# Turning a 128 x 512 map of k: TensorE transposes and ScalarE copies, or VectorE's 32 x 32 transposes

## The chip, the core and the metric

The kernel runs on one core of a Trainium2 chip. The metric is device time in microseconds of one execution; the number given for a kernel is the median of several executions. The engines have short names in the profile: PE is TensorE (PEld its weight loads), DVE is VectorE, ACT is ScalarE, POOL is GpSimd, SP is SyncE, which here only issues transfers. Each engine works through its own list of instructions in order, and a semaphore wait at the head of a list holds everything behind it on that engine.

## The reference

Input x is 2048 x 512. It is normalised per row (xn), and then two branches are computed and multiplied:

```
xn = layernorm(x)
q, k, v = xn@wq, xn@wk, xn@wv          # 32 heads of 16, 4 segments of 512 rows
per segment s, per head:
    a_dot = softmax(q k^T / 4 + causal mask) v
    a_mem = (phi(q) M) / (phi(q) z + 1e-6)      # phi(t) = t + 1 if t > 0 else exp(t)
    o     = g a_mem + (1 - g) a_dot             # g = sigmoid(beta), per head
    M    += phi(k)^T v ;  z += sum over rows of phi(k)
s_out = concat(o) @ wo
h     = relu(xn @ w1) @ w2               # w1 512 x 1792, w2 1792 x 512
out   = x + s_out * silu(h)
```

What matters for the change is the line for M. It sums over the rows of a segment, so on TensorE the rows have to lie on the partitions, for phi(k) as for v.

## The kernel before

All large products are split in two parts (`h` and `l` tiles) and are made of three matmuls each, in two halves of 64 partitions that run side by side in the array: the lower half at L742, the upper half at L750. One such pair of matmuls over 512 columns is called a step below. Weights are loaded by SP into `io` tiles, split by ACT (L408) and POOL (L409).

The four segments are cut into four groups of 8 heads each, so there are 16 groups n = 4s + g. For a group, `proj` computes q and k, `projout` splits them for a transfer to DRAM and back (`stack`), and makes phi of q and k (L982, L983 on ACT, L990 on DVE). Half a group (4 heads) at a time goes through `rowmax` (scores at L1144 on TensorE, their row maxima at L1150 on DVE, in five steps of PSUM tiles), `maxrows` (a 32-partition transpose of the maxima at L1168 on DVE and two transfers), `expo` (transposed scores at L1196, exponentials on ACT at L1207 and L1213) and `pv` (L1244). The feed-forward branch is the filler between these.

The work around the change is this. phi(k) of a group is a tile `pk` of 128 partitions (8 heads x 16) by 512 rows. `memory(n)` turns it into `pkT`, 128 rows on the partitions, four chunks of 128 columns. `memory2(n)` multiplies it with v (32 small matmuls at L1101) and adds the result into `mc` (L1106, L1109). The last segment needs no map, so `memory` works for 12 groups. Before the change it takes two PSUM banks, makes 8 TensorE transposes of 64 partitions (L1071, two side by side), and copies the two banks into `pkT` with two ACT instructions (L1077). There is one `pkT` buffer.

PSUM has eight banks: six general ones, taken one or two at a time by the steps, `rowmax`, `pv` and `memory`, and a pair `pt` for `expo` and `numden`.

What sets the order: the program first collects all work as a list of small entries (an entry is one call of `S.pe`, `act`, `dve`, `pool` or `dma`; `Tape.op` and `Tape.pe` only append to the list). Then `Tape.play` issues them in the order that the string ORDER writes out: each letter says which of the waiting entries, counted from the back of the list, comes next. The duration that a call carries (0.14 + 140 x 0.00105 us for a call of `dve` with 140 columns, say) is not used when the kernel is built; such durations belonged to the search that wrote the strings. CHOICES holds the yes and no decisions of the program (among them how many warming matmuls stand in the opening, and when a chain is flushed without a partner), BANKS the PSUM bank of each taking, PLAN the order of the weight loads.

## Time and profile before

| quantity | value |
|---|---|
| median of 3 executions | 704.0 us (703.73 to 704.62) |
| the profiled execution's own time | 705.35 us |
| its span, first to last instruction | 703.6 us |
| granted TensorE clock | 1.00 |
| PE busy | 688.4 us (98%) |
| DVE busy | 438.4 us (62%) |
| ACT busy | 415.6 us (59%) |
| POOL busy | 448.0 us (64%) |

The busy times are unions of instructions: two matmuls side by side count once. Matmul ends are modelled, so a busy PE is not PE at its peak, and a short wait can hide in it. A row of a group reads: line, engine, operation, tiles, shapes, count, then busy time and mean of one, then the idle time of that engine ahead of it and what ended it.

### The profile page before, as it was taken

Reading aid. Unit: us, or ns where it says so; the run is one execution under the profiler, and the core shown is the slowest. Engines: PE = TensorE matmul, PEld = TensorE weight load, DVE = VectorE, ACT = ScalarE, POOL = GpSimd, SP = SyncE. Lnnn points to the kernel's source line nnn. Section 1 sums busy time; section 2 is a strip of 40 time slices with the busy share of each in tenths; the row PEclk is TensorE's granted clock in tenths of the full one; section 3 lists DMA queues with packets and bytes.
Section 4 is the critical chain, followed back from the end, with each engine's and each line's share of the span. In section 5 each row is a group of like instructions: output and inputs, shape, how many; then the busy total and the mean of one; then the engine's idle time right before and its main releaser. Section 6 shows DMA issues by size and latency. Waiting matters only on the chain.

```text
span 703.6 us, 18639 instructions
## 1 busy us (share of the span) xinstructions
PE 688.4 (98%) x6866; PEld 554.8 (79%) x6866; DVE 438.4 (62%) x1399; ACT 415.6 (59%) x645; POOL 448.0 (64%) x571
## 2 busy tenths in 40 slices
PE   9999999999999999999999999999999999999996
PEld 7878788878877798787788769787777878877675
DVE  4078767675966666466666664765577447566156
ACT  5454656756765773665575676457557555664651
POOL 4561656555666657774775777578467666765575
PEclk9999999999999999999999999999999999999999
DMA  5786466556875578666477567867666787745334
GB/s 171 230 277 205 148 219 196 188 178 203 261 226 154 191 234 283 205 193 201 142 242 231 185 200 221 260 200 228 197 184 185 237 273 228 254 149 144 95 86 135
DMA packets 126451, 141.46 MB, mean 201 GB/s; under 512 B 24904, under 2 KB 70216, under 8 KB 126360
## 3 DMA queue, kind: packets, MB, share of 16 engines
q1 hardware_dynamic: 126152, 140.07, 64.5%
q8 instruction: 54, 0.88, 0.5%
q14 instruction: 37, 0.30, 0.1%
q10 hardware_dynamic: 208, 0.20, 0.1%
HBM read 99.01 MB, written 34.93 MB: 190 GB/s over the span
## 4 chain that ended last, share of the span: by engine, by line
PE 89%; DVE 4%; DMA 3%; ACT 2%; issue 1%; SPq 1%; POOL 0%; DVEq 0%; POOLq 0%; ACTq 0%
PE ps L742 48%; PE ps L750 14%; PE ps L1244 10%; PE ps L1144 6%; PE pt L1196 6%; DVE none L1150 1%; DVE F L1033 1%; ACT pq L1031 1%; DMA ks<-sdk 1%; PE pt L1023 1%; DMA dd<-rq 1%; PE ps L700 1%; PE ps L698 1%; PE ps L699 1%; DMA io<-in_A_wv_dram 1%
## 5 line engine op out<-in xcount | busy, mean ns | idle before, releaser
L1150 DVE CUSTOM_DVE_ANT_0 none<-ps,causal 128x512 bf16<-128x512 f32 (+3 forms) x512 | 250.2, 489 | 107.1 <-PE ps L1144 85.6
L409 POOL TENSOR_TENSOR wl<-io,wh 128x512 fp32r<-128x512 f32 x176 | 227.9, 1304 | 114.6 <-ACT wh L408 89.8
L1213 ACT ACTIVATE P<-pt 128x1024 f32<-128x1024 f32 x128 | 131.3, 1026 | 78.2 <-PE pt L1196 56.0
L750 PE MATMUL ps<-xl,wh 64*128 64x512 f32 x352 | 142.2, 404 | 0.0
L742 PE MATMUL ps<-xh,wh 64*128 64x512 f32 x352 | 141.6, 402 | 0.0
L750 PE MATMUL ps<-xh,wh 64*128 64x512 f32 x352 | 137.1, 389 | 0.0
L750 PE MATMUL ps<-xh,wl 64*128 64x512 f32 x352 | 137.0, 389 | 0.0
L742 PE MATMUL ps<-xl,wh 64*128 64x512 f32 x352 | 136.8, 389 | 0.0
L742 PE MATMUL ps<-xh,wl 64*128 64x512 f32 x352 | 136.7, 388 | 0.0
L408 ACT ACTIVATE wh<-io 128x512 fp32r<-128x512 f32 x176 | 106.9, 626 | 41.7 <-PE ps L750 20.3
L1203 POOL TENSOR_SCALAR_AFFINE_SELECT P<-P 128x512 f32<-128x512 f32 x128 | 80.4, 644 | 39.5 <-ACT P L1213 26.8
L742 PE MATMUL ps<-wh,hh 64*128 64x512 f32 x224 | 91.3, 408 | 0.3 <-DVE md L1150 0.3
L750 PE MATMUL ps<-wl,hh 64*128 64x512 f32 x224 | 90.7, 405 | 0.0
L750 PE MATMUL ps<-wh,hl 64*128 64x512 f32 x224 | 87.3, 390 | 0.0
L750 PE MATMUL ps<-wh,hh 64*128 64x512 f32 x224 | 87.2, 389 | 0.0
L742 PE MATMUL ps<-wl,hh 64*128 64x512 f32 x224 | 87.2, 389 | 0.0
L742 PE MATMUL ps<-wh,hl 64*128 64x512 f32 x224 | 87.1, 389 | 0.0
L1144 PE MATMUL ps<-ks,qs 64*128 64x256 f32 (+3 forms) x512 | 74.1, 332 | 3.5 <-issue 1.4
L1244 PE MATMUL ps<-P,vt 128*17 128x512 f32 (+3 forms) x1024 | 75.2, 434 | 0.0
L742 PEld LDWEIGHTS ps<-xh,wl 64*128 64x128 f32 x352 | 65.0, 185 | 8.1
L1196 PE MATMUL pt<-qs,ks 64*128 64x384 f32 (+3 forms) x512 | 67.6, 312 | 3.9 <-DVE F L1033 2.6
L742 PEld LDWEIGHTS ps<-xh,wh 64*128 64x128 f32 x352 | 65.2, 185 | 7.6 <-issue 1.7
(181 smaller groups left out, 1720.8 us busy)
## 6 DMA issues: line engine op xcount, KB each, us to landing
io<-in_B_w_dram SPq DMA_DIRECT2D x112, 256.0 KB
qs<-sdq SPq DMA_DIRECT2D x32, 512.0 KB
ks<-sdk SPq DMA_DIRECT2D x32, 512.0 KB
sdq<-F SPq DMA_DIRECT2D x16, 512.0 KB
sdk<-F SPq DMA_DIRECT2D x16, 512.0 KB
io<-in_A_x_dram SPq DMA_DIRECT2D x28, 256.0 KB
io<-in_A_wv_dram SPq DMA_DIRECT2D x16, 256.0 KB
io<-in_A_wq_dram SPq DMA_DIRECT2D x16, 256.0 KB
```

Of the source, the lines that this page charges most:

```text
L408: act(512, [rk], [hk], lambda: ACT.activation(h, raw, AF.Copy), 7.0 + nsplit if early else 6.0)
L409: pool(512, [rk, hk], [lk], lambda: POOL.tensor_tensor(l, raw, r32(h), op=OP.subtract), 8.5 + 1.3 * nsplit if early else 25.4)
L698: PE.matmul(pt, st_, mv_, start=first, stop=False)
L699: PE.matmul(pt, st_, ml, start=False, stop=False)
L742: i = PE.matmul(m[0], m[2][0][LO], m[2][1][LO], start=m[4], stop=False)
L750: PE.matmul(h[0], h[2][0][HI], h[2][1][HI], start=False, stop=h[5] is not None)
L1144: PE.matmul(two[a][0][:, o:o + w], qs[r, p, w - 128:w], ks[r, p, :w], start=True, stop=True)
L1150: dve(w + 40 + TTR, [pk, "causal"], [f"{dk}.{p}{a}{j}"], lambda p=p, j=j, o=o, w=w, a=a, pS=pS: DVE.tensor_tensor_reduce(none[:, :w], pS[: ...
L1196: PE.matmul(pT[:, a, o:o + w], ks[r, p, 128 * i:128 * i + 128], qs[r, p, 128 * i:], start=True, stop=True)
L1203: pool(512, ks, ks, lambda: POOL.affine_select(t, t, pattern=[[0, 4], [1, 128]], compare_op=OP.is_ge, fill=0.0, base=0, channel_multiplier ...
L1213: act(1024, tk, [both[p]], lambda: ACT.activation(P[:, 2 * p:2 * p + 2, :], pT, AF.Exp, scale=0.25), 18.5)
L1244: PE.matmul(pO[32 * b:32 * b + 17, 128 * i:], v, P[:, b, o:o + w], start=i == 0, stop=i == 3)
```

## The change

`memory(n)` no longer asks for PSUM banks. In place of the 8 TensorE transposes and 2 ACT copies it issues 16 DVE transposes. Each reads 32 partitions of `pk` (32 features, b = 0 to 3) by 128 columns (32 rows out of each of the four chunks, picked by a = 0 to 3) and writes 32 partitions of `pkT`, in four blocks of 32 x 32. Each has its own key, so that `memory2` waits for all 16. The content of `pkT` is the same.

The four strings are written anew. PLAN is as long as before (176 loads, a few changed in place). BANKS has 909 entries instead of 933, 24 fewer, which is two for each of 12 maps. ORDER has 4,014 entries instead of 3,858, 156 more; 12 x (16 - 1 - 2) is 156, since the 8 TensorE transposes were one entry. The first 96 decisions of CHOICES, which take in all those on warming matmuls in the opening (19 times yes, 20 times no), are the same bit for bit.

```diff
@@ -55,62 +55,63 @@
 CHOICES = (
-    "fffbc60001aab2ab2abaaeaafa01041efb7ac3ac75dd9f77b3f6f3d023beeee2773b38ef73bf773fe5f7cf9e815f7def7bb3b9d8ee0f2777"
...
+    "fffbc60001aab2ab2abaaeaaba01041ebedd93ac75ddbdbecbf67c5ddc082777673bb1cef73bfef79f95fbcf8fbdeeabbe1dd8eee87f0fbbb"
...
 PLAN = (
-    "IJKLQAERSTUVefghBFWXCGYZijklDHabcdmnopAEQRqrSBFIJKLTUVCefghGWXDHMNOPYZijklaAEbcdmnopQRBFqrSTIJKLUVefghCGWXMNOPDH"
+    "IJKLQAERSTUVefghBFWXYCGZijklDaHbcdmnopAEQRqrSBFIJKLTUVCGefghWXYDHMNOPZijklabAEcdmnopBFQRqrSTIJKLUVefghCGWXMNOPDH"
     "YZijklaAEbcdmnopBFQRqrSTIJKLCGMNOPUVefghDHWXYZijklabcdmnopqrMNOP")
...
@@ -1062,25 +1063,18 @@
         if s == NSEG - 1:
             return
         pk, fk, zs, z = PK.pop(n)
-        yield ask(*fk, 2)
-        two = PDR.take(2)
-
-        def go():
-            for c in range(4):
-                for (pt, _), r in zip(two, HALF):
-                    PE.transpose(pt[:, 64 * c:64 * c + 64], pk[r, 128 * c:128 * c + 128], ident[r, r])
-
-        S.pe(T64, fk, [k for _, k in two], go)
         assert not PKTS
         pkT, tk = PKT.next()
-        for (pt, pk_), r in zip(two, HALF):
-            act(256, [pk_], [tk], lambda pt=pt, r=r: ACT.activation(
-                pkT[:, :, r], pt[:, :256].rearrange("p (c f) -> p c f", c=4), AF.Copy), 0.0)
-        PKTS[n] = (pkT, tk, zs, z)
-        yield 0.45, False
+        tks = [f"{tk}.{a}{b}" for a in range(4) for b in range(4)]
+        pv = pk.rearrange("p (t a j) -> p a t j", a=4, j=32)
+        for i, k in enumerate(tks):
+            a, b = slice(32 * (i // 4), 32 * (i // 4) + 32), slice(32 * (i % 4), 32 * (i % 4) + 32)
+            dve(140, fk, [k], lambda a=a, b=b, i=i: DVE.transpose(pkT[a, :, b], pv[b, i // 4]), 4.0)
+        PKTS[n] = (pkT, tks, zs, z)
+        yield 0.0, False
 
     def memory2_needs(n):
-        return [PKTS[n][1], *(f"v{vbuf(n)}{c}" for c in range(4))], [PDR.two()[0][1]]
+        return [*PKTS[n][1], *(f"v{vbuf(n)}{c}" for c in range(4))], [PDR.two()[0][1]]
```

## The prediction

> **What bounds the kernel now.** I read the page's sums and its chain first, then the busy times of TensorE by stretch, then what TensorE waits for.

> ```profile
> span 703.6 us, 18639 instructions
> PE 688.4 (98%) x6866; PEld 554.8 (79%) x6866; DVE 438.4 (62%) x1399; ACT 415.6 (59%) x645; POOL 448.0 (64%) x571
> PE 89%; DVE 4%; DMA 3%; ACT 2%; issue 1%; SPq 1%; POOL 0%; DVEq 0%; POOLq 0%; ACTq 0%
> ```

> ```profile
> 0.00:10.00 10.00, 8.30 (x47) 7.87 (x48) 3.24 (x12) 5.00 (x10) 3.02 (x10) 1.00 0.55 184
> 10.00:692.00 682.00, 674.13 (x6791) 542.24 (x6792) 428.42 (x1376) 409.38 (x632) 439.18 (x553) 1.00 0.66 202
> 692.00:704.00 12.00, 5.94 (x31) 4.74 (x29) 6.77 (x12) 1.25 (x4) 5.83 (x10) 0.96 0.40 137
> ```

> The columns of the second fence are the stretch, its length, then the busy times of PE, PEld, DVE, ACT and POOL, then clock, DMA share and GB/s. TensorE is idle for 1.7 us in the first 10 us, 6.1 us in the last 12, and 7.9 us in the 682 us between. 89% of the chain that ends last is TensorE's. No other engine is above 64%. So what is taken from TensorE comes off the end nearly one for one, as long as the idle time stays as it is. The waits that TensorE still has on DVE are these (total us, times, longest):

> ```profile
> PE pt L1196 <- DVE F L1033: 2.6, 7, 0.5
> PE ps L1144 <- DVE hl L783: 0.7, 1, 0.7
> PE ps L1144 <- DVE md L1150: 0.3, 1, 0.3
> PE ps L742 <- DVE md L1150: 0.3, 1, 0.3
> ```

> That is 3.9 us, and 2.6 of it belongs to the denominators of `numden`, where TensorE waits for the one result that it asked for. Only 1.3 us come from a DVE that had other things to do first.

> **The change part by part.**

> **TensorE loses the 8 transposes of each map.** Their price is read from the timeline of one map (start, duration):

> ```profile
> 99.91 0.40 PE L742 MATMUL ps<-wh,hl 64*128 64x512 f32 x1
> ...
> 100.14 0.41 PE L1071 MATMUL ps<-ident,pk 64*128 64x64 f32 x8
> 100.36 0.47 PE L742 MATMUL ps<-wh,hh 64*128 64x512 f32 x1
> ...
> 100.67 0.38 PE L742 MATMUL ps<-wl,hh 64*128 64x512 f32 x1
> ...
> 100.90 0.39 PE L742 MATMUL ps<-wh,hl 64*128 64x512 f32 x1
> ```
> ```profile
> L1071 PE MATMUL ps<-ident,pk 64*128 64x64 f32 x96 | 5.1, 225 | 0.0
> ```

> Steps start 0.23 us apart (100.67 to 100.90). The transposes take the place from 100.14 to 100.36, 0.22 us, and the step behind them takes 0.31 instead of 0.23, 0.08 more. One map costs TensorE 0.30 us and 12 cost 3.6 us. The bounds are 12 x 0.22 = 2.6 us, if the slow step stays for another reason, and the 5.1 us of the group's busy time. I take 3.6. The number of TensorE entries is otherwise unchanged: ORDER grows by 156 = 12 x 16 - 12 - 24, so no chain is flushed without a partner more or less often than before, and the warming decisions are the same. The rest of TensorE's work is the same work in another order.

> **ACT loses 24 copies, PSUM two holdings per map.**

> ```profile
> L1077 ACT ACTIVATE pkT<-ps 128x256 f32<-128x256 f32 x24 | 8.9, 384 | 3.3 <-PE ps L1071 3.2
> ```

> ACT does 8.9 us less. It is idle 41% of the span, and TensorE has no wait on L1077, so I take 0 for both, with no loss possible and a gain that is inside the bounds of the new order below.

> **DVE gains 192 transposes.** The profile has no transpose of this shape. The nearest rows are the transpose of the row maxima, 128 partitions by 32 columns, and the four widths of the row maximum, which show what 128 more columns cost:

> ```profile
> L1168 DVE STREAM_TRANSPOSE mT<-mm 128x32 f32<-128x32 f32 x32 | 6.6, 208 | 9.8 <-POOL mm L1159 9.8
> L1150 DVE CUSTOM_DVE_ANT_0 none<-ps,causal 128x512 bf16<-128x512 f32 x128 | 88.3, 690 | 59.4 <-PE ps L1144 54.4
> L1150 DVE CUSTOM_DVE_ANT_0 none<-ps,causal 128x256 bf16<-128x256 f32 x128 | 53.8, 420 | 12.1 <-PE ps L1144 6.6
> L1150 DVE CUSTOM_DVE_ANT_0 none<-ps,causal 128x128 bf16<-128x128 f32 x128 | 37.0, 289 | 21.5 <-PE ps L1144 16.5 <-PE pt L1196 0.2
> ```

> From 128 to 512 columns the time rises by 401 ns, 1.04 ns a column. A transpose of 128 columns is then 208 + 96 x 1.04 = 308 ns, an estimate. The lower bound is 208 ns (the same operation, fewer columns), the upper one 420 ns (a row of twice the width). So one map is 16 x 0.308 = 4.9 us of DVE, and all are 59 us (40 to 81). The row speaks of a large fixed part: 208 ns with only 33 ns of columns in it, some 175 ns, paid 16 times. [...]

> These transposes lie between the end of phi(k) and the matmuls that read the map:

> ```profile
> L990 DVE SCALAR_TENSOR_TENSOR pk<-ps,pk x12: 627/688/692, 37.1 to 443.2; 128x512 f32<-128x512 f32 x12
> L1101 PE MATMUL ps<-vt,pkT x384: 192/196/218, 64.8 to 497.5; 128*32 128x32 f32 x192
> ```

> The first map is ready for turning at 37.8 us (37.1 plus 0.69) and read at 64.8, 27 us later; the last one at 443.9 and 497. The 4.9 us fit in there, so the length of the chain through the map costs nothing. What hides them is DVE's idle time between 38 and 500 us:

> ```profile
> 38.00:500.00 462.00, 455.44 (x4828) 369.88 (x4826) 308.49 (x1019) 283.89 (x444) 297.34 (x391) 1.00 0.68 210
> ```
> ```profile
> DVE none L1150 <- PE ps L1144: 85.6, 88, 4.3
> ```

> DVE is busy 308.5 of 462 us (67%) and would be busy 367 (79%). The second fence is the largest reason for its idle time: DVE is there before the scores are, 88 times. Work put into these holes costs nothing. If it isn't put there, what gets late is the reading of PSUM banks, L1150 first, and TensorE waits for the banks. Busy over idle time goes from 308.5 / 153.5 = 2.0 to 367.5 / 94.5 = 3.9. If the 1.3 us of waits on a busy DVE grow in that ratio, they grow by 1.2 us. The other end is 0. I take the middle, +0.6.

> **A new wait.** The first transpose into `pkT` waits on DVE until `memory2` of the group before has read the only buffer; before, ACT's copy had this wait. Behind it on DVE stand L1150 and L783, and TensorE waits for those. The two ends are 0, with the entry placed behind that moment, and the price of the slower rival below. I take 0, since 27 us are there to place it.

> **The new order of everything.** What it can win is bounded by the 7.9 us of TensorE idle between 10 and 692 us; half of that, 4 us, is as far as I go to both sides. The value I take is 0, as nothing in the profile says which way.

> **The sum.** -3.6 + 0.6 = -3.0 us. The profiled execution took 705.35 us, 1.35 above the median of 704.0 and 1.7 above its span; the change is counted on the span, and so on the median alike: 704.0 - 3.0 = 701.0 us. With the bounds of the first and third term, from 704.0 - 5.1 = 698.9 to 704.0 - 2.6 + 1.2 = 702.6.

> **The rivals.**

> **The new order wins more.** If half of the 7.9 us of idle time goes too, the time is 704.0 - 3.6 - 4 = 696.4. For it: two banks fewer are held for each map, and TensorE's idle time is in few large pieces. Against it: only 3.9 us of these waits are DVE's, and 1.7 + 6.1 us at the two ends don't depend on the middle.

> **The gain is hidden.** If the chain of a head group (scores, maxima, transfers, exponentials) sets the rate, and the feed-forward steps only fill it, then less TensorE work makes larger holes and the time stays at 704.0. For it, from the chain of waits:

> ```profile
> 65.59 7.20 DMA ks<-sdk
> 399.89 6.29 DMA dd<-rq
> ```

> At these places the chain leaves TensorE for a transfer of 6 to 7 us. Against it: a chain with 11% outside TensorE, while TensorE itself is idle 7.9 us in 682, means that the fill covers nearly all of it; a hole of 3.6 us more in the same places would need the fill to run out.

> **Slower: the transposes of a map stand in one run ahead of a row maximum.** Then DVE is 4.9 us late for a pair of banks.

> ```profile
> 38.00:500.00 462.00, 188.94 (x763) 1.00 0.68 210
> ```

> These are L1150's instructions in the same stretch, 763 with the reads of the accumulator, so some 381 maxima, or 119 steps of `rowmax` (16 maxima are five steps), one every 3.9 us. TensorE needs the pair again about one step later, so of 4.9 us some 1.0 us are left, and DVE, with 153.5 / 119 = 1.3 us idle per step, needs four steps to catch up. With 12 such maps the time is 704.0 - 3.6 + 12 = 712.4, with six 706.4. It decides from 0.3 us a map on, a delay of DVE of 4.2 us. At the upper price of 6.7 us a map (16 x 0.42) it would be 2.8 us a map. For it: DVE goes to 79% in that stretch, and the 180 to 200 us stretch has no room for a map at all:

> ```profile
> 180.00:200.00 20.00, 20.00 (x196) 15.95 (x195) 17.67 (x57) 14.99 (x27) 13.65 (x16) 1.00 0.93 286
> ```

> DVE is busy 17.67 of 20 us there. Against it: the transposes are 16 entries that can stand one by one between maxima, and 27 us are there for each map. [...]

> **How the numbers follow.** What a measurement of this kernel can tell from no change is about 0.2%, 1.4 us: faster is below 702.6, slower above 705.4. I give the forecast 0.46, the better order 0.20, the hidden gain 0.16 and late transposes 0.18. Faster is the first two, 0.66; the same 0.16; slower 0.18. The range reaches from the better order's 696.4 to six late maps at 706.4; beyond lie the all-late case and an order that wins over 4 us.

> **What would show it.** Right: the group at L1071 is gone and TensorE's busy time is 3.6 to 5.1 us lower; STREAM_TRANSPOSE has 192 more, of about 308 ns, and DVE is at some 497 us; ACT at some 407; TensorE's idle between the first 10 and the last 12 us stays near 8 us; waits of TensorE on DVE stay under 5 us. Wrong: TensorE's idle time, or its waits on L1150 and L783, grow by more than 4 us; transposes take over 420 ns or under 208; or TensorE is less idle than before by several us, so that the order, not the transposes, made the time.

## The result, and the profile after

The kernel after takes 709.23 us (708.85 to 710.65), the kernel before beside it 704.31 us. The ratio is 1.0069 with a 95% interval of 1.0045 to 1.0093: 4.9 us slower, where 3.0 us less were forecast, and 2.8 us beyond the upper end of the range. Two executions far out of line, 3,846 us in experiment 4 and 959 us in experiment 5, are in the medians given there and not in the ratios.

The profiled execution of the kernel after took 708.85 us. First come the page's sums and its chain:

```profile
span 707.1 us, 18584 instructions
PE 691.2 (98%) x6770; PEld 558.5 (79%) x6770; DVE 498.1 (70%) x1591; ACT 407.4 (58%) x621; POOL 447.9 (63%) x571
PE 78%; DVE 11%; POOL 3%; ACT 3%; issue 2%; DMA 1%; SPq 1%; DVEq 0%; ACTq 0%; POOLq 0%
```

TensorE has 96 matmuls fewer (6,866 to 6,770), and yet is busy 2.8 us longer. DVE has 192 instructions and 59.7 us more, ACT 24 instructions and 8.2 us less. DVE's share of the chain went from 4% to 11%. By stretch (length, then busy times of PE, PEld, DVE, ACT, POOL, then clock, DMA share, GB/s):

```profile
10.00:692.00 682.00, 673.38 (x6677) 543.27 (x6676) 482.06 (x1560) 399.81 (x605) 435.04 (x550) 1.00 0.66 202
692.00:707.10 15.10, 9.21 (x47) 7.01 (x45) 11.09 (x19) 2.18 (x6) 8.56 (x12) 0.96 0.41 140
38.00:500.00 462.00, 454.75 (x4680) 366.67 (x4678) 363.22 (x1195) 274.74 (x418) 296.09 (x387) 1.00 0.68 208
```

In the middle 682 us TensorE is idle 8.6 us (7.9 before). So the loss isn't idle time that this view shows, and it isn't the clock, which is 1.00 there. The ends of matmuls are modelled, so short waits can lie inside the busy time. DVE is busy 363 of 462 us, 79%, as forecast. The groups that changed (busy, mean ns, idle before), and then the waits (total us, times, longest):

```profile
L1072 DVE STREAM_TRANSPOSE pkT<-pk 32x128 f32<-32x128 f32 x192 | 58.1, 303 | 8.4 <-PE ps L1095 4.4
```
```profile
PE ps L1138 <- DVE hl L784: 2.7, 1, 2.7
PE pt L1190 <- DVE F L1034: 1.1, 3, 0.4
PE ps L743 <- DVE md L1144: 1.1, 3, 0.5
PE ps L1138 <- DVE md L1144: 1.0, 4, 0.3
```
```profile
PEld ps L1138 <- DVE md L1144: 3.9, 11, 0.6
PEld ps L1138 <- DVE hl L784: 3.6, 3, 3.2
```
```profile
DVE none L1144 <- PE ps L1138: 36.8, 43, 3.0
```

L1138 is now the score matmul of `rowmax`, L1144 its row maximum, L784 the split of the feed-forward branch. DVE waited for the scores 88 times, 85.6 us, and now does so 43 times, 36.8 us. Only part of that is the work of the transposes, since with the new order and no map at all (experiment 1) it waits this long:

```profile
DVE none L1144 <- PE ps L1138: 55.9, 65, 3.6
```

So 19.1 us of these holes went to the transposes; 29.7 us less come with the new order alone. But the scores now wait for DVE: for L784 and L1144 before L1138 and L743, 2.7 + 1.1 + 1.0 us, against the 1.3 us of the prediction's fence, and the weight loads with them, 3.9 + 3.6 us. One wait of the list is large. It stands in TensorE's timeline here:

```profile
44.99 0.39 PE L751 MATMUL ps<-xh,wh 64*128 64x512 f32 x1
48.13 0.32 PE L1138 MATMUL ps<-ks,qs 64*128 64x128 f32 x1 [2.74 <-DVE hl L784]
```

It isn't the answer, since nearly the same wait, 2.1 us, is also there in a kernel that loses nothing (experiment 9).

### The profile page after: what moved, and what is told of

It is laid out like the page before. It is cut to its first block, busy times and chain, and to the rows that moved or that the text cites. A ratio compares the mean times of both kernels' runs of the same rounds, so it can differ in the third digit from the quotient of the medians.

```text
span 707.1 us, 18584 instructions
## 1 busy us (share of the span) xinstructions
PE 691.2 (98%) x6770; PEld 558.5 (79%) x6770; DVE 498.1 (70%) x1591; ACT 407.4 (58%) x621; POOL 447.9 (63%) x571
## 4 chain that ended last, share of the span: by engine, by line
PE 78%; DVE 11%; POOL 3%; ACT 3%; issue 2%; DMA 1%; SPq 1%; DVEq 0%; ACTq 0%; POOLq 0%
PE ps L743 40%; PE ps L751 12%; PE ps L1238 9%; PE ps L1138 5%; PE pt L1190 5%; DVE none L1144 4%; DVE pkT L1072 3%; POOL wl L410 2%; DVE F L1034 1%; DMA nn<-F 1%; PE pt L1024 1%; ACT pq L1032 1%; PE pt L474 1%; PE ps L699 1%; PE ps L701 1%
## 5 line engine op out<-in xcount | busy, mean ns | idle before, releaser
L1144 DVE CUSTOM_DVE_ANT_0 none<-ps,causal 128x512 bf16<-128x512 f32 (+3 forms) x512 | 249.6, 488 | 61.2 <-PE ps L1138 36.8
L743 PE MATMUL ps<-xh,wh 64*128 64x512 f32 x352 | 140.9, 400 | 1.0 <-DVE md L1144 0.7
L743 PE MATMUL ps<-xl,wh 64*128 64x512 f32 x352 | 136.7, 388 | 0.0
L743 PE MATMUL ps<-xh,wl 64*128 64x512 f32 x352 | 136.6, 388 | 0.0
L743 PE MATMUL ps<-wh,hh 64*128 64x512 f32 x224 | 92.0, 411 | 0.4 <-DVE md L1144 0.4
L743 PE MATMUL ps<-wl,hh 64*128 64x512 f32 x224 | 87.1, 389 | 0.0
L743 PE MATMUL ps<-wh,hl 64*128 64x512 f32 x224 | 87.0, 388 | 0.0
L1138 PE MATMUL ps<-ks,qs 64*128 64x512 f32 (+3 forms) x512 | 78.3, 337 | 4.1 <-DVE hl L784 2.7
L743 PEld LDWEIGHTS ps<-xh,wh 64*128 64x128 f32 x352 | 65.0, 185 | 9.6 <-issue 2.9
L743 PEld LDWEIGHTS ps<-xh,wl 64*128 64x128 f32 x352 | 64.8, 184 | 7.4
```

The costliest lines, as they stand in the source:

```text
L743: i = PE.matmul(m[0], m[2][0][LO], m[2][1][LO], start=m[4], stop=False)
L1138: PE.matmul(two[a][0][:, o:o + w], qs[r, p, w - 128:w], ks[r, p, :w], start=True, stop=True)
L1144: dve(w + 40 + TTR, [pk, "causal"], [f"{dk}.{p}{a}{j}"], lambda p=p, j=j, o=o, w=w, a=a, pS=pS: DVE.tensor_tensor_reduce(none[:, :w], pS[: ...
```

## The experiments

Theory L was that DVE's load makes the loss, theory O that the new order does. Ratios are against the kernel before, run beside each.

**1 and 2. The new order, and the old order, with no map at all.** Both leave the map out (`pkT` is zeroed once), with every wait, entry and PSUM bank as it was.

```diff
-            dve(140, fk, [k], lambda a=a, b=b, i=i: DVE.transpose(pkT[a, :, b], pv[b, i // 4]), 4.0)
+            dve(140, fk, [k], lambda: None, 4.0)
```

> The changed kernel with its 192 transposes left out and pkT filled with zeros once at the start, so that the sums M of the memory branch are left out of the result; order and all else as in the changed kernel. Theory L (the 58 us of transposes make DVE late, so PSUM banks are read late and TensorE waits): the 7 us that TensorE's waits grew go away, 701 to 703 us. Theory O (the transposes are hidden, and the new order of everything else is the worse one): 707 to 709 us, as with them.

In the second one, TensorE's transposes and ACT's copies are left out of the kernel before:

```diff
         def go():
-            for c in range(4):
-                for (pt, _), r in zip(two, HALF):
-                    PE.transpose(pt[:, 64 * c:64 * c + 64], pk[r, 128 * c:128 * c + 128], ident[r, r])
+            pass
...
-            act(256, [pk_], [tk], lambda pt=pt, r=r: ACT.activation(
-                pkT[:, :, r], pt[:, :256].rearrange("p (c f) -> p c f", c=4), AF.Copy), 0.0)
+            act(256, [pk_], [tk], lambda: None, 0.0)
```

> The kernel before with the 8 TensorE transposes and 2 ACT copies of each map left out and pkT filled with zeros once, so that the sums M are left out of the result; order as before. It measures the first term of the sum by itself. Both theories: 704.3 - 3.6 = 700.7 us, 699 to 702. If the time stays at 704, TensorE's saving is worth nothing in this order either.

The new order without its map takes 701.54 us (0.9965, 0.9949 to 0.9981), the old one 702.10 us (0.9975, 0.9956 to 0.9994). Theory L's range holds for the first; the second is 0.1 us above the range that both theories gave. So the order isn't the cause: the two differ by 0.6 us in medians, and the intervals overlap. The map on TensorE and ACT costs 2.1 us in medians, with an interval of 0.4 to 3.1 us; the spans of the two profiles are 3.9 us apart (703.6 and this):

```profile
span 699.7 us, 18415 instructions
PE 685.3 (98%) x6770; PEld 562.9 (80%) x6770; DVE 439.9 (63%) x1399; ACT 408.9 (58%) x621; POOL 449.1 (64%) x572
```

The map on DVE costs 709.23 - 701.54 = 7.7 us. The two traces have the same order, so their matmuls can be matched one by one: the kernel after is behind by 1.5 us at 50 us, by 4.1 at 150, by 5.4 at 250, and by 5.4 at the end. In this pair the delay is made before 250 us.

**3. The old order, with the transposes at the places of ACT's copies.** Eight in a row, twice a map.

```diff
+        def turn8(h):
+            for i in range(8 * h, 8 * h + 8):
+                a, b = slice(32 * (i // 4), 32 * (i // 4) + 32), slice(32 * (i % 4), 32 * (i % 4) + 32)
+                DVE.transpose(pkT[a, :, b], pv[b, i // 4])
+
+        for h in range(2):
+            act(256, [two[h][1]], [tk], lambda h=h: turn8(h), 0.0)
```

> The kernel before, same order of everything, with the map turned by the 16 DVE transposes, 8 at the place of each ACT copy, and TensorE's transposes gone. Theory O: 700.7 to 702 us, as the old order is the good one. Theory L: 8 transposes in a run are 2.5 us of DVE ahead of what waits behind; 24 such runs cost at least what was saved, 704 to 709 us.

It takes 737.91 us (1.0478, 1.0446 to 1.0511), far above the 709 us that theory L allowed. This is nearly the prediction's slower rival carried out, with a map in two runs in place of one, and it shows the price: against experiment 2, which has the same order, (737.91 - 702.10) / 12 = 3.0 us a map. DVE's timeline and then TensorE's, at one map:

```profile
450.25 2.50 DVE L1079 STREAM_TRANSPOSE pkT<-pk 32x128 f32<-32x128 f32 x8
452.78 0.56 DVE L1154 CUSTOM_DVE_ANT_0 none<-ps,causal 128x384 bf16<-128x384 f32 x1
453.26 0.08 DVE L1154 DVE_READ_ACCUMULATOR2_ANT md<- 128x1 f32 x1
453.38 2.53 DVE L1079 STREAM_TRANSPOSE pkT<-pk 32x128 f32<-32x128 f32 x8
455.94 0.29 DVE L1154 CUSTOM_DVE_ANT_0 none<-ps,causal 128x128 bf16<-128x128 f32 x1
456.15 0.08 DVE L1154 DVE_READ_ACCUMULATOR2_ANT md<- 128x1 f32 x1
```
```profile
451.96 0.28 PE L1148 MATMUL ps<-ks,qs 64*128 64x256 f32 x1
456.29 0.50 PE L1148 MATMUL ps<-ks,qs 64*128 64x256 f32 x3 [4.05 <-DVE md L1154]
```

DVE spends 2.50 + 2.53 = 5.0 us on the map, and TensorE stands still from 452.2 (one step of 0.23 us after 451.96) to 456.3, 4.1 us. The cover at this map is 0.9 us, not the 3.9 us of the rival.

After the long stall the matmuls are slower, too (L742 takes 0.62 us at 457.07, 0.39 at 451.73). By stretch:

```profile
448.00:456.00 8.00, 4.24 (x65) 3.16 (x63) 7.11 (x26) 3.89 (x6) 4.13 (x5) 1.00 0.39 118
456.00:460.00 4.00, 3.71 (x23) 3.71 (x25) 2.60 (x12) 1.02 (x1) 0.48 (x1) 0.61 0.13 25
```

The granted clock in the 4 us after the stall is 0.61, which is half clock for 3.1 of the 4 us. The spell goes on to 460.3, 3.4 us in all. The clock falls to half around the end of five other stalls of this run, which last 3.6, 2.3, 3.5, 1.8 and 2.3 us, and not at two of 1.9 and 1.5 us; in the kernel after the 2.7 us of idle time at 45 us drew no such drop. So the length of a stall alone doesn't decide here: one of 1.8 us drew a drop, those of 1.9 and 2.7 us drew none. What does decide, no run shows. The profiled span is 35.0 us longer than that of the kernel before (738.6 and 703.6). TensorE is idle for 23.0 us more and busy for 12.0 us more, and the six spells of half clock, 23.9 us together, are by estimate worth about those 12 us.

**4. The old order, with the transposes spread into DVE's idle places.** The 16 transposes of a map were taken out of their place and issued at chosen positions of ORDER, where the trace of before shows DVE idle; TensorE's transposes and ACT's copies are left out as in 2.

```diff
+TURNS = {
+    196: ((0, 0), (0, 1), (0, 2), (0, 3), (0, 4), (0, 5), (0, 6), (0, 7), (0, 8), (0, 9), (0, 10), (0, 11), (0, 12), (0, 13), (0, 14), (0, 15)),
+    354: ((1, 0), (1, 1), (1, 2), (1, 3), (1, 4), (1, 5)),
+    408: ((1, 6), (1, 7), (1, 8), (1, 9)),
...
+        p = 0
         for c in code:
+            for n, i in TURNS.get(p, ()):
+                MAPS[n](i)
+            p += 1
```

> The kernel before, same order of everything else, with the 16 DVE transposes of a map put one by one or in runs ahead of DVE instructions before which DVE had been idle, as long as the idle time lasts (map 0 has 3.5 us of it for 4.9). Theory O: 700.7 to 702 us. Theory L in the form that load alone decides: 704 to 708 us; in the form that only the place decides: 701 to 703 us, below e3.

709.77 us (1.0078, 1.0054 to 1.0102), above the range of either form of theory L, and the same as the kernel after within the noise, with another order, other places, and a longer wait on the single buffer (9.7 us, 4.4 in the kernel after):

```profile
DVE pkT L1148 <- PE ps L1173: 9.7, 8, 3.4
```

Two very different orders thus give the same time, so spreading the transposes into idle places doesn't bring the old order's time back. That no placement would is not shown, and here the wait on the buffer can be part of the price.

**5 and 6. As 4, with one half of the maps on DVE, the other on TensorE.** Maps 0 to 5 first, then maps 6 to 11; the edit is the table TURNS alone, with the entries of those maps.

> The kernel before with its order; maps 0 to 5 (up to about 230 us) turned by DVE at the places of the run that put all transposes into idle time, maps 6 to 11 by TensorE and ACT as before. Theory early (DVE's load costs in the first 250 us, where DVE was busy 70% and the maps follow each other every 33 us, and later nothing): 708 to 710 us. Theory even (each map on DVE costs the same): half of the 5.6 us lost there, 706 to 708 us.

> The kernel before with its order; maps 0 to 5 by TensorE and ACT as before, maps 6 to 11 (from about 240 us on) by DVE at the places of the run that put all transposes into idle time. Theory early: 702.5 to 704.5 us, no dearer than TensorE's maps. Theory even: 706 to 708 us.

With maps 0 to 5 on DVE the time is 711.19 us (1.0084, 1.0057 to 1.0111), with maps 6 to 11 it is 703.81 us (0.9987, 0.9974 to 1.0000). The first is 1.2 us above its range of theory early, the second within it. In the old order the whole price is in the first six maps, before 250 us; the last six can be on either engine. What makes it there these two runs don't settle, since DVE also stands longer at the single buffer in the first of them (3.3 us in the second, in four waits):

```profile
DVE pkT L1122 <- PE ps L1147: 6.4, 4, 3.4
```

The stretches 38 to 250 and 250 to 500 us of the second one:

```profile
38.00:250.00 212.00, 208.96 (x2254) 168.73 (x2251) 157.75 (x532) 134.29 (x212) 128.14 (x187) 1.00 0.66 203
250.00:500.00 250.00, 247.35 (x2549) 203.88 (x2548) 180.97 (x585) 147.83 (x223) 168.37 (x205) 1.00 0.71 217
```

DVE is busy 74% in the first, which has no transposes on DVE, and 72% in the second, which has them. This is the fastest kernel of the study that computes the whole map, but within 0.2% of the kernel before.

**7. Transposes that stay in their own 32 partitions.** In the kernel after, each of the 16 transposes reads one group of 32 partitions and writes one, and no two of them have the same pair of groups. This kernel has the same number of transposes in the same order, over 128 partitions at once and with no shift between groups. The map it makes is another one: no block leaves its partitions.

```diff
-            dve(140, fk, [k], lambda a=a, b=b, i=i: DVE.transpose(pkT[a, :, b], pv[b, i // 4]), 4.0)
+            dve(140, fk, [k], lambda a=a, b=b, i=i: DVE.transpose(pkT[:, :, b], pv[:, i // 4]), 4.0)
```

> The changed kernel, its order and its 192 DVE transposes, but each over all 128 partitions and within its own 32, so that no instruction reads one group of 32 partitions and writes another; the map is then not the right one, and the sums M are left out. If the load of DVE decides: 708 to 710 us, as the changed kernel. If the change of partitions holds DVE up (instructions that don't overlap the one ahead): up to 192 x 0.08 us = 15 us of DVE less, and 704 to 707 us.

702.27 us (0.9971, 0.9955 to 0.9988), better than the 704 to 707 us expected if the change of partitions holds DVE up. The whole loss is gone, with the same 192 transposes of 300 ns:

```profile
L1072 DVE STREAM_TRANSPOSE pkT<-pk x192: 253/300/314, 37.6 to 497.7; 128x128 f32<-128x128 f32 x192
```

The duration of one is the same (a median of 303 ns in the kernel after), but they overlap. Eight in a row in DVE's timeline, first here, then in the kernel after:

```profile
37.60 1.97 DVE L1072 STREAM_TRANSPOSE pkT<-pk 128x128 f32<-128x128 f32 x8
```
```profile
37.00 2.52 DVE L1072 STREAM_TRANSPOSE pkT<-pk 32x128 f32<-32x128 f32 x8
```

That is 0.25 us for each here and 0.315 us there. In the kernel after each that stands right behind another starts 14 ns behind its end, here 76 ns ahead of it (medians of the trace).

**8. Short transposes, with the shift.** Is it the holding of the starts itself that costs, or DVE's time? This kernel keeps the groups of the kernel after and turns one 32 x 32 block in place of four, so three quarters of the map are left out (`pkT` is zeroed once in 8, 9 and 10, as in 1).

```diff
-            dve(140, fk, [k], lambda a=a, b=b, i=i: DVE.transpose(pkT[a, :, b], pv[b, i // 4]), 4.0)
+            dve(140, fk, [k], lambda a=a, b=b, i=i: DVE.transpose(pkT[a, 0, b], pv[b, i // 4, 0]), 4.0)
```

> The changed kernel, its order and its 192 transposes, but each of one block of 32 x 32 instead of four, so that three quarters of the map are zeros and that part of the sums M is left out. A transpose should take about 0.2 us, 40 us of DVE instead of 58. If the price goes with DVE's time: 701.5 + 7.4 x 40/58 = 706.6 us. If it goes with the number of instructions: 708 to 710 us. If DVE's spare time decides with a threshold: below 704 us.

703.24 us (0.9973, 0.9956 to 0.9989), with starts that are held just as much (14 ns behind the end, none overlaps):

```profile
L1072 DVE STREAM_TRANSPOSE pkT<-pk x192: 189/203/208, 37.0 to 499.6; 32x32 f32<-32x32 f32 x192
```

So the holding as such costs 1 us or less in medians: DVE's total time is close to that of 7, and so is the kernel's. What held starts do to the kernel after they do by way of DVE's time.

**9, 10 and 11. What in the groups holds a start.** Experiment 7 changed the shift, the change between neighbours and the width together. The ninth keeps 32 x 128 and uses the first group alone for input and output; the tenth keeps input and output in the same group and lets that group change from one to the next; both make another map. The eleventh makes the whole map, with the roles of input and output exchanged.

```diff
 # 9
+            dve(140, fk, [k], lambda a=a, b=b, i=i: DVE.transpose(pkT[:32, :, b], pv[:32, i // 4]), 4.0)
 # 10
+            dve(140, fk, [k], lambda a=a, b=b, i=i: DVE.transpose(pkT[b, :, a], pv[b, i // 4]), 4.0)
 # 11
+            a, b = slice(32 * (i % 4), 32 * (i % 4) + 32), slice(32 * (i // 4), 32 * (i // 4) + 32)
+            dve(140, fk, [k], lambda a=a, b=b, i=i: DVE.transpose(pkT[a, :, b], pv[b, i % 4]), 4.0)
```

> The kernel after, with all 16 transposes of a map reading the first 32 partitions of pk and writing the first 32 of pkT, so that neither the input nor the output group changes from one to the next. It leaves the true map out: pkT holds other data. Same count, same shape of 32 x 128, same order, no shift of partitions. The run without partition shift differed from the kernel after in three things: no shift, no change of group, and 128 partitions wide. If the change of group between consecutive instructions is the price: starts 0.25 us apart inside a run of transposes, DVE busy about 480 us, and a time of 702 to 704 us. If 32 partitions instead of 128 are the price: 708 to 710 us and 0.31 us apart.

> The kernel after, with each transpose reading and writing the same group of 32 partitions, and another group in each consecutive transpose. The map is wrong: only the blocks stay in their own partitions. If the change of group from one instruction to the next is the price: as the kernel after, 0.31 us apart, DVE busy about 498 us, 708 to 710 us. If the shift of partitions inside one instruction is the price: 702 to 704 us, 0.25 us apart.

> The kernel after, with the 16 transposes of a map in another order: four consecutive ones read the same 32 partitions of pk and write a different group of pkT each (in the kernel after, four consecutive ones write the same group and read a different one each). The map is complete. If a change of the input's group alone holds the next instruction, three of four starts are freed: DVE busy about 484 us, 702 to 705 us. If a change of either end holds it, nothing changes: 708 to 710 us.

The ninth takes 702.59 us (0.9969, 0.9953 to 0.9985), the tenth 706.28 us (1.0026, 1.0011 to 1.0041), outside both of its ranges, the eleventh 709.87 us (1.0072, 1.0048 to 1.0096). Eight in a row, of 9, then 10, then 11:

```profile
37.53 1.93 DVE L1072 STREAM_TRANSPOSE pkT<-pk 32x128 f32<-32x128 f32 x8
```
```profile
37.05 2.28 DVE L1072 STREAM_TRANSPOSE pkT<-pk 32x128 f32<-32x128 f32 x8
```
```profile
37.03 2.52 DVE L1072 STREAM_TRANSPOSE pkT<-pk 32x128 f32<-32x128 f32 x8
```

The width isn't it: 32 partitions overlap (0.24 us each) when the group stays. For the rest one has to know that ORDER issues the 16 in a shuffled order (3, 13, 11, 5, 9, 1, 14, 4 and so on for the first map), which the expectation of the eleventh overlooked: it doesn't free three starts of four, it only changes which end moves. So the pairs of neighbours are counted, those of the trace in which a transpose stands right behind another (the input's group is i mod 4 in the kernel after, the output's is i div 4):

| from one transpose to the next | kernel | pairs | overlap |
|---|---|---|---|
| input's group stays, output's changes | after | 16 | 0 |
| output's group stays, input's changes | after | 16 | 0 |
| both change | after | 45 | 0 |
| both change | 10 | 59 | 0 |
| both stay | 10 | 16 | 16 |
| both stay, other columns written | 9 | 63 | 63 |
| both stay, same columns written again | 9 | 19 | 0 |

Here a change at either end holds the next one (none of the 136 pairs with a change overlaps), also when there is no shift between input and output inside one instruction (the tenth); whether a shift without a change would hold it no run shows. Where no group changes the starts overlap, but for those of the ninth that write over what the one in front has just written. The tenth has 16 of 75 pairs free, and its time lies between. A whole map can't have two neighbours with the same groups at both ends, since each of its 16 transposes has another pair; by these counts no other order of the 16 frees a start right behind another. What the holding costs, the fences of 9 and 11 show: 0.08 us for each start (2.52 - 1.93 = 0.59 us over the seven starts behind the first). The row maxima pay as well: one that stands right behind a transpose starts 31 ns behind its end in the kernel after and 64 ns ahead of it in the ninth (medians over 47 such pairs each). In all DVE is busy 498.1 - 478.7 = 19.4 us longer than in the ninth, 0.10 us for each transpose.

**DVE's time and the end.** The kernels with the new order and 6,770 matmuls differ only in what DVE does for the map:

| kernel | DVE busy, whole span, us | DVE busy, 38 to 250 us | time, us |
|---|---|---|---|
| 1, no map | 442.7 | 157.5 | 701.54 |
| 7, no change of group, 128 wide | 478.7 | 174.6 | 702.27 |
| 9, one group | 478.7 | 173.9 | 702.59 |
| 8, short, held | 481.4 | 173.8 | 703.24 |
| 10, held in part | 494.0 | 177.1 | 706.28 |
| after | 498.1 | 179.3 | 709.23 |
| 11, output group changes | 498.5 | 179.5 | 709.87 |

```profile
38.00:250.00 212.00, 208.02 (x2198) 170.33 (x2196) 173.88 (x632) 130.29 (x199) 124.54 (x180) 1.00 0.64 203
```
```profile
38.00:250.00 212.00, 206.50 (x2152) 166.78 (x2150) 179.31 (x614) 127.12 (x194) 119.58 (x178) 1.00 0.64 200
```

The two rows are of 9 and of the kernel after. In 7 and 9 the first 36 us of DVE work cost 0.7 and 1.0 us, hardly clear of the noise; the next 20 cost 6.6: it is a bend, not a line. In the first 250 us the bend lies between 82% (173.9 of 212) and 85% (179.3) of DVE busy. That the load of the stretch is what bends it is argued, not shown: the length of every run of transposes changes along with it, and with the old order experiment 5 takes 711.19 us at 178.0 us of 212, more than the kernel after at 179.3. Where the 6.6 us are on TensorE shows between these two kernels, which have the same matmuls. The ninth's sums:

```profile
span 701.0 us, 18579 instructions
PE 686.7 (98%) x6770; PEld 553.2 (79%) x6770; DVE 478.7 (68%) x1591; ACT 407.1 (58%) x621; POOL 448.2 (64%) x572
```
```profile
PE ps L1138 <- DVE hl L784: 2.1, 1, 2.1
```

The spans differ by 6.1 us (707.1 and 701.0). 4.5 of them are in "busy" time (691.2 and 686.7), presumably in waits too short to be listed, which the profile doesn't show one by one, and 1.6 in idle time. The one large wait is there in both (2.7 and 2.1 us). Matched one by one, the kernel after is behind the ninth by 2.7 us at 150 us, 4.3 at 250 and 6.1 at the end, so in this pair nearly a third of the delay comes after 250 us.

## Why the prediction was wrong

**TensorE loses the transposes, -3.6.** The group is gone, the count of matmuls is right. The gain was there before the loss came on top: 2.1 us in medians (experiment 2), 3.9 us in the profiled spans. The 3.6 lie just outside the interval of 0.4 to 3.1; how the rest is made up, if it is, the runs don't settle. That TensorE's busy time would fall by 3.6 to 5.1 us was wrong: where only the map was left out it fell by 3.1 (experiment 2, 688.4 to 685.3), and in the kernel after it rose by 2.8, since most of the new delay lies in it.

**ACT and PSUM, 0.** ACT did 8.2 us less. Experiment 2 takes this relief together with TensorE's, 2.1 us for both, so that it has no large gain of its own.

**DVE's work, 308 ns and 59 us.** Right: 303 ns and 58.1 us, and 79% of the stretch.

**DVE's load, +0.6, bounds 0 and 1.2.** This is the step that failed. The term measured +7.7 us. Its basis was wrong twice. It took the 1.3 us of listed waits and let them grow with busy over idle time; but only part of the delay shows as listed waits, and against the ninth 4.5 of 6.1 us lie in TensorE's busy time. And it took one mean over 38 to 500 us, where most of the price comes in the first 250 us (experiments 5 and 6, and the matched traces). The holes of DVE before the row maxima were a cover for some of it: 19.1 us of them went to the transposes (55.9 to 36.8). That "work put into these holes costs nothing" came out for the first 36 us only; the 20 us after them, which held starts add, cost 6.6.

**The price of a start.** The prediction priced a transpose by its duration, and the duration was right. It didn't ask whether the transposes overlap. Without the change of group the same 192 add 36 us instead of 55 to DVE, and the time is 702.3 to 702.6 us.

**The new wait on `pkT`, 0.** Right in effect, though the wait came. DVE waits there twice, 4.4 us in all, and just as much in the ninth (4.5 us), which loses nothing.

**The new order, 0.** Right: 701.54 and 702.10 us without the maps.

**The rivals.** The slower one came out on its side, at a time that its own range (706.4 to 712.4) held, but not by its mechanism. Its cover of one step, 3.9 us, is 0.9 us at the map shown of experiment 3, and maps in long runs cost 3.0 us each there, not 1.0. In the kernel after the transposes are spread over many short runs, and the price comes in many small delays. So that the time lies in the rival's range is luck. The hidden gain and the better order fall with experiments 1 and 2. The range failed in ending at "six late maps", a count that stood for no mechanism.

**What made the time.** 704.3 - 2.1 (map off TensorE) - 0.6 (order) + 1.0 (36 us of DVE work, of experiments 7 and 9 against 1) + 6.6 (the 20 us more that held starts make) = 709.2. These are differences along one chain of medians, so they must add up; the 0.6 and the 1.0 are not clear of the noise.

## What to carry to other kernels

In this kernel an engine that returns PSUM banks to TensorE could be filled up to a point at almost no price and then quickly cost much (0.7 to 1.0 us for the first 36 us of DVE work, 6.6 us for the next 20). So read such a load in its fullest stretch, not over the span alone, and look for the bend by leaving the new work out or shortening it. Short delays of TensorE need not show in its idle time or in the list of waits (4.5 of 6.1 us here stood in its busy time); compare the busy time of the same matmuls. Before VectorE takes many small instructions, see whether neighbours use the same group of 32 partitions: where they didn't here (the kernel after), a transpose started 14 ns behind the end of the one before, and where they did (experiment 7), 76 ns ahead of it, in medians.
